# Attention products on pairs of 64x64 array tiles, and a triangle inversion by columns with unit steps on VectorE

## Chip, cores, metric

The kernel runs on one core of one Trainium2 chip. The metric is device time in microseconds, lower is better: 2314.84 us is the median of three runs of the kernel before (2313.5 to 2316.09). The words TensorE, VectorE, ScalarE, GpSimd and SyncE stand for the rows PE, DVE, ACT, POOL and SP of the profile; PEld is TensorE's weight load.

## What is computed

A layer in three parts; the first is a recurrence over 768 steps for 32 independent heads (4 batches of 8) of width 48.

```python
k_n = k / (np.linalg.norm(k, axis=-1, keepdims=True) + 1e-06)
for t in range(S):                      # S = 768
    y[:, :, t] = q_t @ state            # state: 48 x 48 for each of 32 heads
    v_old = state' k_t
    state = state + beta_t * outer(k_t, v_t - v_old)
x = y as (3072, 384)
P = exp(x @ w_gate), scaled 8 times over rows and columns; out = sum_e P[:, e] * (relu(x @ w1[e]) @ w2[e])
result = ((out @ a) * (out @ b) @ w3) @ w_out      # float64 weights
```

## The kernel before, in words

**Attention.** The 768 steps are cut into 12 chunks of 64. Two batches lie on the two halves of the 128 partitions (64 steps each), and the other 16 heads (`NG`) lie along the free axis, in two halves `hf` of 8. In a chunk the recurrence is a triangular system: `T' = (I + diag(beta) L)^-1 diag(beta)` is made from the products of keys, then `u = T'(v - K S)` and `S += K^T u`. Every value is kept as two fp16 parts, so each product is three matmuls (high x high, high x low, low x high). Because the two batches of a partition pair are independent, the stationary operand of such a product has to be block diagonal, 128 x 128 with two blocks of 64: the tiles `ktexp` (keys transposed), `ttexp` (T'), `kexp` (keys) and `bx` (u and state) hold zeros beside the blocks. They are filled in three ways: `ktexp` by copies on VectorE or ScalarE (`prep_k`, line 338 or 336), `ttexp`, `kexp` and `bx` by DMAs on SyncE's queue (line 363) from the compact tiles `tt16`, `k16`, `u16` and `s16`; the first chunk's `ttexp` and `bx` by copies.

**Order in a pair of chunks.** `prep_k` normalises the keys, splits them, transposes them on TensorE (`i,k` in the rows), and multiplies them with themselves (`gram`, rows `ktc,ktexp`). `invert(j)` inverts the 32 x 32 diagonal triangles of two chunks at once: 128 partitions, 32 triangles each after a 32 x 32 stream transpose (lines 620, 672, 674). It solves blocks of 8 by seven substitution steps (a product and a sum, lines 343 and 630), then joins blocks of 8 to 16 and of 16 to 32 by products with broadcast operands of 512 or 1024 elements followed by a sum (lines 343 and 643). The second operand of a product is read with a step of a whole row of 32. Four of the ten joins of a pair take their product on GpSimd. `tt_make` joins the two 32-halves of each 64-triangle with 32 x 32 TensorE tiles (rows `asys,g` and `stg,g`, `tile_position`) and makes `tt16`. `prep_q` makes the queries and `P^T` (rows `q,ktexp`). `seq(c)` is the recurrence: `ks` (rows `s,ktexp`), `um` (`r,ttexp`), `um2` (`u,kexp`) and `ym` (`q,bx` and `pt,bx`), with ScalarE and VectorE splitting what comes out of PSUM. The chunk's rows of x go to DRAM and back as `xr`.

**Filler and the rest.** `e0(c)` multiplies a finished chunk with the first expert's blocks (rows `xr,wA` and `hA,wA`, 256 columns): 144 matmuls a chunk for ten chunks. It has the lowest priority, so TensorE takes it where the attention waits. Then come the scaling of the gate (`sinkhorn`, lines 1048 to 1070), the other experts and the last layers, all matmuls of 256 to 512 columns.

**What sets the order.** A planner (`Plan.order`) lists all operations engine by engine from their data dependences, priorities, estimated costs and rings of buffers; each engine then runs its list in order. The single ring for `g12` makes a pair's `gram` wait for the `tt_make` of the pair before it, and the ring of two for x makes `e0(c)` finish before chunk c + 2 gets its x.

Of the kernel before, what the change touches and what calls it, by code (L numbers as in the profile page):

```python
# [17 lines left out]
NCH = 12  # L18
# [10 lines left out]
NKX = 1  # L29
NA0 = 2  # L30
NKC = 2
NBX = 2
# [3 lines left out]
NTC = 1  # L36
# [4 lines left out]
TSL = 1  # L41
ULAT = 1.0
# [5 lines left out]
DIRECT = 1  # L48
UDIRECT = 1
KX3 = 1  # L50
NG12 = 1
ZDVE = (("k16", 0), ("ktexp", 0))
ZPOOL = (("k16", 1), ("ktexp", 1))
# [3 lines left out]
class Ring:  # L57
    """Interchangeable buffers, each taken by one value at a time, with a cap per class of value."""
# [24 lines left out]
class Plan:  # L83
    """Operations with their data dependences; `order` lists them engine by engine with estimated costs."""
# [49 lines left out]
    def wait_for(self, o, e, pool, now, room):  # L134
        """Whether a more urgent operation will want the engine in a moment."""
        for x in pool:
            if x is o:
                return False
            if x.prio[0] < self.URGENT and e in x.rdy and len(x.engs) == 1 and now < x.rdy[e] <= now + self.AHEAD and x.engs[e] <= 2 * o.engs[e]:
                t = room(x)  # L140
                if t is not None and t <= now + self.AHEAD:
                    return True
        return False

    def order(self):
# [14 lines left out]
        def cost_of(o, e):  # L160
            """The tensor engine runs at half rate after a window of little work, until one of much work."""
# [148 lines left out]
class Kernel:  # L310
# [19 lines left out]
    # -- small helpers -------------------------------------------------  # L330
# [35 lines left out]
    # -- setup ---------------------------------------------------------  # L366
    def setup(self):
# [12 lines left out]
                  k16=((128, K16, 2, 2, 8, 64), F16), kexp=((128, NKX * 3584 + 16), F16), ktexp=((128, KSL, 2, 2, 8, 128), F16),  # L380
                  q16=((128, NQ, 2, 8, 64), F16), pt=((128, NPT, 2, 8, 64), F16),
                  ttexp=((128, TSL, 2, 2, 8, 128), F16), vs=((128, NV, NG, D), F32),
                  s16=((128, 2, 2, 8, D), F16), r16=((128, 2, 2, 8, D), F16), u16=((128, 2, 2, 8, D), F16),
                  bx=((128, NBX * 3584 + 16), F16))
        self.open("xst", "left", xst=((128, NY, 2, 512), F32))
        self.open("prep", "right",
                  kraw=((128, NG, D), F32), qraw=((128, NG, 64), F32), ktc=((128, NKC, 2, 8, 64), F16), tt16=((128, NTC, 2, 2, 8, 64), F16),
# [24 lines left out]
        def zero(name, i, key, n, prio):  # L412
            dst = lambda: self.wide(name)[:, i] if name in ("kexp", "bx") else T[name][:, i]
            if (name, i) in ZDVE:
                g.op({"DVE": n / 1900 + .07}, lambda e: nc.vector.memset(dst(), 0.0), w=[(key, i)], prio=prio)
            elif (name, i) in ZPOOL:
                g.op({"POOL": n / 1200 + .07}, lambda e: nc.gpsimd.memset(dst(), 0.0), w=[(key, i)], prio=prio)
            else:
                self.dma(lambda: dst().rearrange(FLAT), lambda: a["zeros"][:, 0:n], 256 * n, [], [(key, i)], prio)
        for i in range(K16):  # L420
            zero("k16", i, "kz", 2048, (-9, -8, 8, 8)[i])
        for i in range(KSL):
            zero("ktexp", i, "ktz", 4096, (-8.5, -7.5, 8, 9, 9)[i])
        for nm, n, key in (("kexp", NKX, "xz"), ("bx", NBX, "bz")):
            g.op({"POOL": .1}, lambda e, nm=nm, n=n: nc.gpsimd.memset(T[nm][:, 3584 * n:], 0.0), w=[(key, "z")], prio=1.3)
        for i in range(NKX):
            zero("kexp", i, "xz", 3584, 1.5)
        for i in range(TSL):
            zero("ttexp", i, "ttz", 4096, 1.4)
        for i in range(NBX):  # L430
            zero("bx", i, "bz", 3584, 1.6 + .1 * i)
# [7 lines left out]
        self.kxring = Ring(range(NKX), fifo=True)  # L439
        self.ktcring = Ring(range(NKC), fifo=True)  # L440
        self.bxring = Ring(range(NBX), fifo=True)
        self.stg = Ring(range(NST))
        self.kraw = Ring([0], fifo=True)
# [5 lines left out]
        self.ttring = Ring(range(TSL), fifo=True)  # L449
# [10 lines left out]
    # columns of `sml`  # L460
# [3 lines left out]
    def scale_chain(self, src, dst, inv, bits, prio, key):  # L464
        """From a column of row sums of squares: the power of two 2**bits over the root of their sum, and its inverse."""
# [22 lines left out]
    def vscan(self):  # L488
        """sv: power of two that bounds the scaled values and the state."""
# [12 lines left out]
    # -- attention, what does not depend on the state -------------------  # L502
    def prep_k(self, c):
# [3 lines left out]
        raw = ["asys"] if c == 1 else [("s16", hf, i) for hf in range(2) for i in range(2)] if c == 3 and KX3 else [self.kraw.new()]  # L507
        kraw = lambda: (T["asys"][:, 0:768] if c == 1 else T["s16"].rearrange("p h i y d -> p (h i y d)").bitcast(F32)).rearrange(
            "p (g d) -> p g d", d=D) if c == 1 or c == 3 and KX3 else T["kraw"]
# [33 lines left out]
        ktz = [("ktz", i) for i in range(KSL) if i == c or c >= KSL]  # L543
# [3 lines left out]
        for hf in range(2):  # L547
            gs = slice(8 * hf, 8 * hf + 8)
            kt = self.ktcring.new()
            for i in range(2):  # L550
                s = self.psum.new("attn")

                def tr(e, i=i, hf=hf, s=s):
                    o = self.ps(s, 4, 128)
                    for x in range(4):
                        self.mm(o[:, x], T["k16"][:, kc.at, hf, i, 2 * x:2 * x + 2].rearrange("p y d -> p (y d)"), T["i128"],
                                start=True, stop=True)
                g.op({"PE": 4 * .056}, tr, r=[(kc, "hl"[i], hf), "i128"], w=[s, (kt, i)], prio=pr)
                g.op({"ACT": act(512, True), "DVE": dve(512)},
                     lambda e, i=i, kt=kt, s=s: self.copy(e, T["ktc"][:, kt.at, i], self.ps(s, 8, 64)),  # L560
                     r=[s], w=[(kt, i)], prio=pr)
                for b in range(2):
                    r = slice(64 * b, 64 * b + 64)
                    g.op({"DVE": dve(512, 4), "ACT": act(512)},
                         lambda e, i=i, hf=hf, b=b, r=r, kt=kt: self.copy(
                             e, T["ktexp"][r, k.at, hf, i, :, 64 * b:64 * b + 64], T["ktc"][r, kt.at, i]),
                         r=[(kt, i)] + ktz, w=[(k, "t", hf, i, b)], prio=pr)
            s = self.psum.new("attn")

            def gram(e, hf=hf, s=s, kt=kt):  # L570
                o = self.ps(s, 8, 64)
                for x in range(8):
                    th, tl = T["ktexp"][:, k.at, hf, 0, x], T["ktexp"][:, k.at, hf, 1, x]
                    ch, cl = T["ktc"][:, kt.at, 0, x], T["ktc"][:, kt.at, 1, x]
                    self.mm(o[:, x], th, ch, start=True, stop=False)
                    self.mm(o[:, x], th, cl, start=False, stop=False)
                    self.mm(o[:, x], tl, ch, start=False, stop=True)
            g.op({"PE": 24 * .029}, gram, r=[(kt, 0), (kt, 1)] + [(k, "t", hf, i, b) for i in range(2) for b in range(2)],
# [932 lines left out]
```

## Time and profile before

| | |
|---|---|
| median of three runs | 2314.84 us (2313.5 to 2316.09) |
| span of the profiled execution | 2309.9 us |
| what lies around the span, taken from the median | 4.9 us |
| TensorE, VectorE, ScalarE, GpSimd busy | 2157.7, 1356.5, 711.7, 422.3 us |
| SyncE's queue (q1) | 292992 packets, 150.88 MB |

The page gives the span of one execution; its time from outside is not given apart, so the 4.9 us between span and median are used for it. Busy times are shares of the whole span, and the span has two very different stages: attention with filler up to about 500 us, then matmuls alone. A stage is therefore read from the windows, not from the page's totals. In the timeline a group of matmuls ends with the end of its last one, which is modelled; the time that a group takes from TensorE is from its start to the start of the next group.

### The profile page before, as it was taken

What the parts mean: (1) busy time and instruction counts of PE and PEld (TensorE: products, weight loads), DVE (VectorE), ACT (ScalarE), POOL (GpSimd) and SP (SyncE); (2) the same over time, 40 slices, a digit from 0 to 9 for tenths busy, and PEclk for the clock granted to TensorE, in tenths of its full rate; (3) what the DMA queues carried; (4) which work ended last, traced back from release to release, by engine and by line L of the source; (5) the groups of instructions that cost most, each with busy time, mean ns of one, the idle gap of its engine ahead of it and who ended that gap; (6) DMA issues with size and microseconds to landing.
All of it is one profiled execution on the core that took longest, in us unless ns stands there. A gap on an engine that the chain in (4) does not pass through costs nothing.

```text
span 2309.9 us, 38847 instructions
## 1 busy us (share of the span) xinstructions
PE 2157.7 (93%) x16055; PEld 1894.3 (82%) x16055; DVE 1356.5 (59%) x2350; ACT 711.7 (31%) x1415; POOL 422.3 (18%) x351
## 2 busy tenths in 40 slices
PE   2488888899999999999999999999999999999999
PEld 1477877789788888888888888888888888999999
DVE  8989888865877777777544444444444444222332
ACT  4645665554223222223121211212111111223332
POOL 5554456343211101111000000000000001300000
PEclk7579998999999999999999999999999999999999
DMA  6446545544523323233110101101010033500000
GB/s 218 123 90 108 107 94 115 87 97 151 172 87 119 107 79 108 93 113 112 53 42 19 42 27 33 46 14 46 14 46 28 18 127 101 110 18 18 15 15 21
DMA packets 312048, 175.10 MB, mean 76 GB/s; under 512 B 187072, under 2 KB 281600, under 8 KB 310848
## 3 DMA queue, kind: packets, MB, share of 16 engines
q1 hardware_dynamic: 292992, 150.88, 24.1%
q0 software_dynamic: 18880, 21.76, 3.7%
q8 instruction: 125, 2.05, 0.4%
q14 instruction: 51, 0.42, 0.1%
HBM read 123.09 MB, written 31.29 MB: 67 GB/s over the span
## 4 chain that ended last, share of the span: by engine, by line
PE 79%; DVE 14%; DMA 3%; issue 2%; ACT 1%; SPq 1%; POOL 0%; DVEq 0%; ACTq 0%; POOLq 0%
PE b L332 79%; DVE prod L343 3%; DMA ttexp<-tt 2%; DVE t L643 1%; DVE ktexp L338 1%; DVE xs L643 1%; DVE hA L346 1%; SPq L363 1%; DVE r L343 1%; DMA kexp<-k 0%; DVE xr L343 0%; DVE asys L672 0%; DMA pb<-p_d 0%; DVE stg L343 0%; DVE tt L343 0%
## 5 line engine op out<-in xcount | busy, mean ns | idle before, releaser
L332 PE MATMUL b<-xT,wA 128*128 128x512 f32 x2520 | 584.7, 389 | 0.0
L332 PEld LDWEIGHTS b<-xT,wA 128*128 128x128 f32 x2520 | 473.0, 188 | 98.2
L332 PE MATMUL b<-hA,wA 128*128 128x512 f32 (+1 forms) x2286 | 507.4, 361 | 16.1 <-DVE hA L346 15.9
L332 PEld LDWEIGHTS b<-hA,wA 128*128 128x128 f32 x2286 | 391.8, 194 | 78.8 <-DVE hA L346 18.4
L332 PE MATMUL b<-hB,wA 128*128 128x512 f32 (+1 forms) x1602 | 412.2, 384 | 1.0 <-DVE hB L346 1.0
L332 PEld LDWEIGHTS b<-hB,wA 128*128 128x128 f32 x1602 | 296.2, 189 | 60.8 <-DVE hB L346 1.8
L343 DVE TENSOR_TENSOR tmp<-b,pb 128x512 f32<-128x512 f32 x252 | 173.9, 690 | 243.4 <-PE b L332 242.7
L1179 ACT ACTIVATE hA<-b 128x512 fp32r<-128x512 f32 (+1 forms) x174 | 102.7, 590 | 635.3 <-PE b L332 627.8
L346 DVE SCALAR_TENSOR_TENSOR hA<-b,hA 128x512 fp32r<-128x512 f32 (+1 forms) x214 | 145.4, 680 | 179.2 <-ACT hA L1179 156.4
L332 PE MATMUL b<-xr,wA 128*128 128x256 f32 (+1 forms) x1368 | 248.3, 334 | 1.0 <-DVE ktc L338 1.0
L332 PEld LDWEIGHTS b<-xr,wA 128*128 128x128 f32 x1368 | 211.9, 199 | 21.1 <-DVE ktc L338 1.2
L332 PE MATMUL b<-xr,xT 128*128 128x256 f32 x1728 | 209.9, 283 | 0.0
L332 PEld LDWEIGHTS b<-xr,xT 128*128 128x128 f32 x1728 | 209.3, 192 | 0.0
L346 DVE SCALAR_TENSOR_TENSOR hB<-b,hB 128x512 fp32r<-128x512 f32 (+1 forms) x178 | 119.7, 674 | 150.9 <-ACT hB L1179 150.9
L343 DVE TENSOR_TENSOR acc<-acc,tmp 128x512 f32<-128x512 f32 x249 | 181.4, 728 | 6.6
L1179 ACT ACTIVATE hB<-b 128x512 fp32r<-128x512 f32 (+1 forms) x178 | 103.7, 583 | 194.4 <-PE b L332 193.4
L343 POOL TENSOR_TENSOR wA<-rawB,wA 128x768 fp32r<-128x768 f32 x13 | 26.8, 2064 | 659.4 <-ACT wA L336 659.4
L343 DVE TENSOR_TENSOR cv<-b,cv 128x256 f32<-128x256 f32 x96 | 40.7, 423 | 162.2 <-PE b L332 161.7
L343 POOL TENSOR_TENSOR cv<-cv 128x256 f32<-128x256 f32 (+1 forms) x68 | 53.2, 783 | 301.0 <-DVE cv L1276 179.6
L336 ACT ACTIVATE cvs<-cv 128x256 fp32r<-128x256 f32 x72 | 29.0, 402 | 168.4 <-DVE cv L346 168.4
L332 PEld LDWEIGHTS <-ktexp 128*128 128x128 f16 (+1 forms) x1680 | 58.3, 103 | 15.3 <-issue 8.2
L336 ACT ACTIVATE wA<-rawB 128x768 fp32r<-128x768 f32 x56 | 45.9, 841 | 78.6 <-DMA rawB<-in_moe_w 39.6
(191 smaller groups left out, 2247.2 us busy)
## 6 DMA issues: line engine op xcount, KB each, us to landing
pb<-p_d SPq DMA_DIRECT2D x90, 256.0 KB, 3.2
rawB<-in_moe_w SPq DMA_DIRECT2D x112, 192.0 KB, 3.1
w_d<-cvs SPq DMA_DIRECT2D x112, 128.0 KB, 2.5
cvr<-in_w3T SPq DMA_DIRECT2D x32, 256.0 KB, 3.3
xT<-w_d POOLq DMA_DIRECT2D x32, 256.0 KB, 3.5
vs<-in_v SPq DMA_DIRECT2D x18, 384.0 KB, 4.2
qraw<-in_qT SPq DMA_DIRECT2D x12, 512.0 KB, 3.9
cvr<-in_moe_w SPq DMA_DIRECT2D x24, 256.0 KB, 3.3
```

What stands on the lines that cost most here:

```text
L332: self.nc.tensor.matmul(*args, skip_group_check=True, **kw)
L336: self.nc.scalar.activation(out=out, in_=in_, func=AF.Copy, **({} if scale is None else {"scale": scale}))
L338: self.E[eng].tensor_copy(out, in_)
L343: self.E[eng].tensor_tensor(out=out, in0=in0, in1=in1, op=op)
L346: self.nc.vector.scalar_tensor_tensor(out=out, in0=in0, scalar=scalar, in1=in1, op0=op0, op1=op1)
L363: return self.g.op({eng: cost}, lambda _: e.dma_start(out=out(), in_=in_()), r=r, w=w, prio=prio, nbytes=nbytes, lat=lat)
L643: g.op({"DVE": dve(m)}, lambda e: nc.vector.tensor_reduce(out=out(), in_=pv(), axis=AX.X, op=ALU.add), r=[pb], w=wk, prio=pr)
L1179: g.op({"ACT": act(N, True)}, lambda e, s=s, h=h, hx=hx, N=N: nc.scalar.activation(out=self.hv(h, hx, N)[:, 0], in_=self.ps(s, N), func=AF ...
```

## The change

The stationary operands are not spread any more. A product is issued as two 64 x 64 tiles, one for each half of the partitions, on the array's tiles (0, 0) and (64, 64); both halves write the same PSUM bank, partitions 0 to 63 and 64 to 127. `ktexp`, `ttexp`, `kexp`, `bx` and `ktc`, their zeroing, copies and DMAs go; `kt` and `tt16` are read directly, `u16` and `s16` get two buffers each and 16 spare columns (what those give is not used). The inversion keeps the triangle `t` by columns (`p c i`) and the system by rows (`p i q`), so that both operands of a product are read with unit steps; all its products are on VectorE; three copies on ScalarE (`by_rows`) turn parts of `t`. `kraw` gets three buffers. The planner counts a pair of tiles as 0.036 us.

```diff
+    def three(self, o, lh, ll, rh, rl, first=True, last=True):
+        for l, r, st, sp in ((lh, rh, first, False), (lh, rl, False, False), (ll, rh, False, last)):
+            for p in range(2):
+                rows = slice(64 * p, 64 * p + 64)
+                self.mm(o(rows), l(rows), r(rows), start=st, stop=sp, tile_position=(64 * p, 64 * p))
...
                 def tr(e, i=i, hf=hf, s=s):
-                    o = self.ps(s, 4, 128)
-                    for x in range(4):
-                        self.mm(o[:, x], T["k16"][:, kc.at, hf, i, 2 * x:2 * x + 2].rearrange("p y d -> p (y d)"), T["i128"],
-                                start=True, stop=True)
+                    o = self.ps(s, 8, 64)
+                    for y in range(8):
+                        for p in range(2):
+                            r = slice(64 * p, 64 * p + 64)
+                            self.mm(o[r, y], T["k16"][r, kc.at, hf, i, y], T["i128"][r, r], start=True, stop=True, tile_position=(64 * p, 64 * p))
...
-                for b in range(2):
-                    r = slice(64 * b, 64 * b + 64)
-                    g.op({"DVE": dve(512, 4), "ACT": act(512)},
-                         lambda e, i=i, hf=hf, b=b, r=r, kt=kt: self.copy(
-                             e, T["ktexp"][r, k.at, hf, i, :, 64 * b:64 * b + 64], T["ktc"][r, kt.at, i]),
...
             g.op({"DVE": dve(4 * i * i)}, lambda e, pv=pv, i=i: nc.vector.tensor_reduce(
-                out=blk("t")[:, :, i, 0:i], in_=pv(), axis=AX.X, op=ALU.add), r=[pb], w=["t"], prio=pr)
+                out=blk("t")[:, :, 0:i, i], in_=pv(), axis=AX.X, op=ALU.add), r=[pb], w=["t"], prio=pr)
...
-            g.op({eng: dve(m) if eng == "DVE" else 2.72 * m / 1000 + .06}, lambda e: self.tt(
-                e, pv(), left().rearrange("p i (u q) -> p i u q", u=1).to_broadcast([128, ni, nc_, nq]),
-                right().rearrange("p q (c u) -> p u c q", u=1).to_broadcast([128, ni, nc_, nq]), ALU.mult),
+            g.op({"DVE": dve(m) + .08}, lambda e: self.tt(
+                "DVE", pv(), left().rearrange("p i (u q) -> p i u q", u=1).to_broadcast([128, ni, nc_, nq]),
+                right().rearrange("p (u c) q -> p u c q", u=1).to_broadcast([128, ni, nc_, nq]), ALU.mult),
...
+        def by_rows(p, n, o, rk):
+            g.op({"ACT": act(n * n) + .1}, lambda e: self.copy("ACT", rows(p, n), tm()[:, o:o + n, o:o + n].rearrange("p q i -> p i q")),
+                 r=rk + ka, w=["tr", ("tr", p)], prio=pr)
...
-        for b in range(2 if c >= DIRECT else 0):
-            r = slice(64 * b, 64 * b + 64)
-            self.dma(lambda r=r, b=b: T["ttexp"][r, tt.at, :, :, :, 64 * b:64 * b + 64].rearrange("p h i y d -> p (h i y) d"),
...
-                    three(o[:, y], T["ttexp"][:, tt.at, hf, 0, y], T["ttexp"][:, tt.at, hf, 1, y],
-                          T["r16"][:, 0, hf, y], T["r16"][:, 1, hf, y])
-            g.op({"PE": 24 * .025}, um, r=[("r16", 0, hf), ("r16", 1, hf)] + [(tt, b, hf) for b in range(2)],
+                    self.three(lambda r: o[r, y], tv(0, y), tv(1, y), rv(0, y), rv(1, y))
+            g.op({"PE": 24 * PAIR}, um, r=[("r16", 0, hf), ("r16", 1, hf)] + [(tt, i, hf) for i in range(2)],
...
-            expand(ux, "u16", [("u16", i, hf) for i in range(2) for hf in range(2)], pr + .4, ULAT)
```

**SyncE's queue in the middle of the attention.** This queue carries the loads of keys, values and queries and, before, the transfers that spread. Before, from one load of keys to the next:

```order
L363 DMA kraw<-in_k 128x768
L363 DMA ttexp<-tt_111 64x32x64 x2
L363 DMA bx<-u_99 64x32x48 x2
L363 DMA kexp<-k_90 64x16x48 x4
L363 DMA ttexp<-tt_111 64x32x64 x2
L363 DMA vs<-in_v 128x768
L363 DMA bx<-s_97 64x32x48
L363 DMA bx<-s_97 48x32x48
L363 DMA xs_d<-xst 48x8x128 x2
L363 DMA kraw<-in_k 128x768
```

Now:

```order
L358 DMA y_d<-yr 128x256 x6
L358 DMA xs_d<-xst 48x8x128 x2
L358 DMA kraw<-in_k 128x768
L358 DMA xst<-xs_d 128x6x128
L358 DMA vs<-in_v 128x768
L358 DMA qraw<-in_qT 128x1024
L358 DMA kraw<-in_k 128x768
```

Every transfer into `ttexp`, `bx` and `kexp` is gone; the loads and the round trip of x stay.

**VectorE in the second half of an inversion.** The rows with `prod` are products, those with `xs` or `t` the sums that follow. Before (a sum that reads `a_113` follows a product on GpSimd):

```order
L343 TENSOR_TENSOR prod<-asys,t 128x1024
L338 COPY ktexp<-ktc 64x8x64
L343 TENSOR_TENSOR xr<-xst,xr 128x768
L643 TENSOR_REDUCE xs<-prod 128x8x8
L343 TENSOR_TENSOR prod<-asys,t 128x1024
L643 TENSOR_REDUCE xs<-a_113 128x16x8
L643 TENSOR_REDUCE xs<-prod 128x8x8
L343 TENSOR_TENSOR prod<-t,xs 128x1024
L473 TENSOR_SCALAR sml<-b_135 128x1
L643 TENSOR_REDUCE t<-prod 128x8x8
L346 SCALAR_TENSOR_TENSOR hA<-b_136,hA 128x512
L643 TENSOR_REDUCE t<-a_113 128x8x8
```

Now (the products that read `a_109` read what ScalarE's `by_rows` copies left there):

```order
L338 TENSOR_TENSOR prod<-asys,t 128x1024
L333 COPY yr<-b_129 128x256
L616 TENSOR_REDUCE xs<-prod 128x8x8
L338 TENSOR_TENSOR prod<-asys,t 128x1024
L341 SCALAR_TENSOR_TENSOR hA<-b_128,hA 128x512
L616 TENSOR_REDUCE xs<-prod 128x8x8
L338 TENSOR_TENSOR prod<-asys,t 128x1024
L341 SCALAR_TENSOR_TENSOR hA<-b_134,hA 128x512
L616 TENSOR_REDUCE xs<-prod 128x16x8
L338 TENSOR_TENSOR prod<-a_109,xs 128x1024
L616 TENSOR_REDUCE t<-prod 128x8x8
L341 SCALAR_TENSOR_TENSOR hA<-b_129,hA 128x512
```

Six products of 1024 elements stand on VectorE for every pair of chunks instead of four, and the copies into `ktexp` between them are gone.

## Rows read from the trace of the kernel before

**Rows 1.** The page, parts 1 and 4: busy time by engine; shares of the last chain.

```profile
PE 2157.7 (93%) x16055; PEld 1894.3 (82%) x16055; DVE 1356.5 (59%) x2350; ACT 711.7 (31%) x1415; POOL 422.3 (18%) x351
PE 79%; DVE 14%; DMA 3%; issue 2%; ACT 1%; SPq 1%; POOL 0%; DVEq 0%; ACTq 0%; POOLq 0%
```

**Rows 2.** Windows: stretch, length, busy per engine, granted clock, DMA share, GB/s.

```profile
0.00:100.00 100.00, 33.42 (x592) 29.19 (x592) 89.22 (x150) 55.86 (x116) 55.70 (x45) 0.63 0.53 173
100.00:500.00 400.00, 327.22 (x5970) 308.46 (x5967) 342.58 (x520) 224.33 (x455) 203.01 (x129) 0.89 0.51 101
500.00:650.00 150.00, 140.72 (x1207) 127.09 (x1204) 99.43 (x185) 55.72 (x106) 43.02 (x35) 0.98 0.53 148
650.00:2309.00 1659.00, 1656.31 (x8301) 1429.57 (x8299) 825.24 (x1498) 375.79 (x739) 120.60 (x142) 1.00 0.19 57
```

**Rows 3.** Waits of TensorE, 0 to 500 us: us in total, times, longest.

```profile
PE b L332 <- DVE hA L346: 13.2, 8, 4.1
PE b L332 <- DVE asys L672: 13.0, 5, 5.9
PE b L332 <- DMA ttexp<-tt: 12.5, 7, 6.9
PE b L332 <- DMA bx<-u: 2.1, 2, 1.3
```

**Rows 4.** Timeline of TensorE: start, length, line, operation, out<-in, shape, count.

```profile
430.03 1.38 PE L332 MATMUL b<-u,kexp 128*128 128x48 f16 x48
431.25 0.86 PE L332 MATMUL b<-ktc,ktexp 128*128 128x64 f16 x24
431.95 1.38 PE L332 MATMUL b<-s,ktexp 112*128 112x48 f16 x48
...
337.28 1.05 PE L332 MATMUL b<-i,k 128*128 128x128 f16 x16
338.14 0.60 PE L332 MATMUL b<-hA,wA 128*128 128x256 f32 x3
...
533.51 2.32 PE L332 MATMUL b<-xr,wA 128*128 128x256 f32 x18
535.67 2.32 PE L332 MATMUL b<-hA,wA 128*128 128x256 f32 x18
```

**Rows 5.** The same, 32 x 32 tiles: at half clock, then at full clock.

```profile
74.30 2.77 PE L332 MATMUL b<-asys,g 32*32 32x32 f32 x96 [5.88 <-DVE asys L672]
77.22 1.06 PE L332 MATMUL b<-stg,g 32*32 32x32 f32 x32
...
480.88 1.71 PE L332 MATMUL b<-asys,g 32*32 32x32 f32 x96 [1.16 <-DVE asys L672]
482.52 3.64 PE L332 MATMUL b<-hA,wA 128*128 128x256 f32 x18
```

**Rows 6.** Groups of VectorE and GpSimd, 0 to 620 us: busy, mean ns, idle before.

```profile
L338 DVE COPY ktexp<-ktc 64x512 f16<-64x512 f16 x64 | 35.9, 563 | 1.4 <-ACT ktc L336 0.4
L343 DVE TENSOR_TENSOR prod<-asys,t 128x1024 f32<-128x1024 f32 x12 | 31.5, 2627 | 0.1
L343 DVE TENSOR_TENSOR prod<-t,xs 128x1024 f32<-128x1024 f32 x12 | 28.2, 2346 | 0.1
L343 DVE TENSOR_TENSOR prod<-t,xs 128x512 f32<-128x512 f32 x6 | 8.2, 1374 | 0.1
L343 DVE TENSOR_TENSOR prod<-asys,t 128x512 f32<-128x512 f32 x6 | 7.4, 1232 | 0.1
L343 DVE TENSOR_TENSOR prod<-t,asys 128x196 f32<-128x196 f32 x6 | 3.6, 601 | 0.1
L343 POOL TENSOR_TENSOR a<-asys,t 128x1024 f32<-128x1024 f32 x6 | 19.8, 3304 | 2.3 <-DVE t L643 2.3
```

**Rows 7.** Timeline of VectorE in the first inversion.

```profile
28.26 1.23 DVE L343 TENSOR_TENSOR a<-a,bm 128x1024 f32<-128x1024 f32 x1
51.08 1.93 DVE L343 TENSOR_TENSOR prod<-asys,t 128x1024 f32<-128x1024 f32 x1
62.79 3.27 DVE L343 TENSOR_TENSOR prod<-t,xs 128x1024 f32<-128x1024 f32 x1
```

More of the change, by code (lines that the diff above doesn't have):

```diff
@@ L47 @@
 HA = 2
[L48 to L50 removed]
 NG12 = 1
[L52 to L53 removed]
+PAIR = .036
+ZDVE = (0,)
+ZPOOL = (1,)
 FLAT = "p a b c d -> p (a b c d)"
@@ L568, in prep_k, with gram @@
+                g.op({"PE": 8 * PAIR}, tr, r=[(kc, "hl"[i], hf), "i128"], w=[s, (k, i, hf, "z")], prio=pr)
+                g.op({"ACT": act(512, True), "DVE": dve(512)},
+                     lambda e, i=i, hf=hf, s=s: self.copy(e, T["kt"][:, k.at, hf, i], self.ps(s, 8, 64)),
+                     r=[s], w=[(k, i, hf)], prio=pr)
             s = self.psum.new("attn")
-            def gram(e, hf=hf, s=s, kt=kt):
+            def gram(e, hf=hf, s=s):
                 o = self.ps(s, 8, 64)
[L572 to L577, printed above, removed]
@@ new lines, in invert @@
+        xt = lambda p, n: T["xs"][:, p * n * n:(p + 1) * n * n].rearrange("p (c q) -> p c q", c=n)
+        rows = lambda p, n: flat()[:, p * n * n:(p + 1) * n * n].rearrange("p (i q) -> p i q", i=n)
+        def by_rows(p, n, o, rk):
+            g.op({"ACT": act(n * n) + .1}, lambda e: self.copy("ACT", rows(p, n), tm()[:, o:o + n, o:o + n].rearrange("p q i -> p i q")),
+                 r=rk + ka, w=["tr", ("tr", p)], prio=pr)
+        for p in range(2):
+            by_rows(p, 8, 16 * p + 8, ["t"])
@@ new lines, in invert @@
+        for p in range(2):
+            o = 16 * p
+            prod(lambda p=p: xt(p, 8).rearrange("p c q -> p q c"), lambda o=o: am()[:, o + 8:o + 16, o:o + 8],
+                 lambda o=o: tm()[:, o:o + 8, o:o + 8], 8, 8, 8, ["asys", "t"], [("x8", p)])
+        for p in (1, 0):
+            o = 16 * p
+            prod(lambda o=o: tm()[:, o:o + 8, o + 8:o + 16].rearrange("p c i -> p i c"), lambda p=p: rows(p, 8),
+                 lambda p=p: xt(p, 8), 8, 8, 8, [("tr", p), ("x8", p)], [("t8", p)])
@@ new lines, in invert @@
+        out = lambda: tm()[:, 0:16, 16:32].rearrange("p c i -> p i c")
+        for c0 in (0, 8):
+            prod(lambda c0=c0: out()[:, 8:16, c0:c0 + 8], lambda: rows(0, 16)[:, 8:16, :], lambda c0=c0: xt(0, 16)[:, c0:c0 + 8, :],
+                 8, 8, 16, [("tr", 0), ("x16", 0, c0), ("x16", 8, c0)], [("t16", 1, c0)])
+        prod(lambda: out()[:, 0:8, :], lambda: rows(0, 16)[:, 0:8, 0:8], lambda: xt(0, 16)[:, :, 0:8],
+             8, 16, 8, [("tr", 0), ("x16", 0, 0), ("x16", 0, 8)], [("t16", 0)])
@@ L930, in seq @@
                 e, T["xst"][:, xb.at, hf], self.ps(s, 512), self.sc(28 + c)), r=[sy, ("sml", 28 + c)], w=[(xb, hf)], prio=pr + .5)
-        if c < NCH - 1:
-            self.SX = self.bxring.new()
-            expand(self.SX, "s16", [("s16", hf, i) for i in range(2) for hf in range(2)], pr + .4, 0.0)
         for b in range(2):
```

260 lines of the change are left out of this document (91 added, 169 removed).

## Prediction

> **What bounds the kernel now.** I read the page first, then the windows, TensorE's waits, its timeline, and VectorE's groups. The page shows TensorE busy 2157.7 of 2309.9 us and on 79% of the last chain [rows 1]. That is a sum over unlike stages, so the windows come next [rows 2]. From 650 us on TensorE is busy 1656.3 of 1659 us at a clock of 1.00: nothing of the change lies there, and that stage can only start earlier or later. All of TensorE's idle time is ahead of it: 66.6 us in the first 100, 72.8 us from 100 to 500, 9.3 us from 500 to 650. In the first stretch VectorE is busy 89 of 100 us and TensorE waits for the first inversion; from 100 to 500 VectorE is busy 342.6 of 400 us and TensorE 327.2. So the attention runs with two nearly full engines that take turns in waiting for each other. TensorE's waits name VectorE most often (13.2 us for `hA`, 13.0 us for the inverse), and 14.6 us the DMAs that spread `ttexp` and `bx` [rows 3].
>
> The end is therefore TensorE's work plus TensorE's idle time, and I make the sum that way: what the change adds to the work, what it takes from the idle time, what the clock does.
>
> **1. TensorE's work (adds).** Times are from the start of a group to the start of the next [rows 4], at full clock. A full-array product with 48 columns takes 25.4 ns (430.03 to 431.25, 48 of them), one with 64 columns 29.2 ns (431.25 to 431.95, 24), a transposing one with 128 columns 53.8 ns (337.28 to 338.14, 16). By the order there are 1632, 2256 and 192 of these: 41.5 + 65.9 + 10.3 = 118 us. The change issues 8544 tile matmuls, 4272 pairs, of 48 (1632 pairs) or 64 columns (2640 pairs). What a pair costs no row shows. The nearest rows are the 32 x 32 tiles, which also alternate between the two halves of the partitions and write one bank: 96 of them take 1.64 us at full clock, 17.1 ns each, 34.2 ns for two [rows 5]. That is the low end: 4272 x 34.2 = 146 us, +28. The high end is no overlap of the two tiles, each at the price of a full-array product: 1632 x 50.8 + 2640 x 58.4 = 237 us, +119. I take 36 ns, close to the tile rows since they are the same kind of instruction, with a little for the longer stream: 154 us, **+36**.
>
> A rule speaks against this. The 32 x 32 rows show two row groups writing one bank at 17.1 ns an instruction, less than any full-array product above [rows 5]. The Trainium skill (TensorEngine Tiling (Array Packing), Restrictions and Gotchas) says that different row tiles cannot access the same PSUM bank at the same time, and both tiles of a pair here write one bank. By that rule the pairs would cost the high end; where the rows can be compared, they do not bear it out.
>
> **2. TensorE's idle time (takes).** VectorE loses the copies into `ktexp`, 35.9 us [rows 6]. In the inversions 24 products of 1024 took 31.5 + 28.2 = 59.7 us and 12 of 512 took 15.6 us [rows 6]. With unit steps I price them by the only product of that size with a contiguous operand, 1.23 us for 1024 [rows 7], and 0.65 us for half as much: 29.5 + 7.8, a gain of 38 us. The 12 products of 1024 and 12 of 512 that leave GpSimd come back on VectorE: +22.6 us. The small substitution products (0.60 us at 196 elements) I take at 1 us less per inversion, 6 us. Together VectorE does 36 + 38 - 23 + 6 = 57 us less. GpSimd loses 19.8 us of 1024-products alone [rows 6], and with them some of the times when a VectorE instruction is stretched: a product of 1024 took 1.93 us at one place and 3.27 us at another [rows 7].
>
> Of that, 100 to 500 us gets about five sixths, 48 us: VectorE's load falls from 342.6 to about 295, below TensorE's. The DMA waits (14.6 us) vanish with the DMAs. I take the idle time there from 72.8 to 30 us, **-43**: 14.6 from the DMAs, the rest from the waits for VectorE and GpSimd [rows 3]. Ends: 14.6 alone, or 60. In the first 100 us the first `um` waits for keys, one inversion and the copies into `ktexp` and `ttexp`; with about 2.5 us less in four large products, 3 us of copies ahead of it and as much behind, and shorter stretched steps I take **-12** (5 to 25).
>
> Against this stand new waits. VectorE's products with `by_rows` operands wait for three ScalarE copies a pair, queued in order behind evacuations of filler; ScalarE is busy only 224 of 400 us [rows 2], and three waits of a microsecond in six inversions would be 18 us of VectorE, not of TensorE. At the end, cover is lost: 504 filler matmuls stood behind the last `um`, now 288 do. At 120 ns each (533.51 to 535.67, 18 of them) [rows 4] that is 26 us less to hide the gate's scaling, which runs on VectorE between small matmuls. The next expert's blocks can fill most of it; I take **+5** (0 to 20). The zeroing, 110 spreading DMAs and their place in SyncE's queue I cost at nothing beyond the waits named; loads of keys, values and queries behind them can only start earlier.
>
> **3. The clock (takes).** A granted clock of 0.89 over 400 us is 88 us at the lower level, 1.2 GHz; at 82% busy and half speed that loses some 36 us [rows 2]. In the first stretch (0.63) filler starts only when the first chunk is done, so an earlier start also ends that cold stretch earlier. Fewer waits should give about half of this back: **-20** (from -30 to +30, since tile products may do the opposite, see the second rival).
>
> **Sum.** 2309.9 + 36 - 43 - 12 + 5 - 20 = 2276 us of span. The 4.9 us around the span, which link it to the median of 2314.84, give 2281 us; I say **2280 us**, 1.5% faster. A measurement of this kernel can tell 0.2%, some 4.6 us, from no change.
>
> **Rivals.**
> - *The tiles do not overlap.* Each pair costs two products: +119 instead of +36, and with TensorE then fuller the idle time falls no further: about 2280 + 83 - 8 = 2355 us, slower. It decides in the attention products; the gains of 70 us are used up at a pair price of (118 + 70) / 4272 = 44 ns. For it: at half clock the 32 x 32 tiles take at most 28.9 ns each (96 in 2.77 us) [rows 5], and 32 columns alone are 26.7 ns at 1.2 GHz, so those rows fit one tile after the other too, if an fp32 instruction passes 32 columns once. Against: 17.1 ns is well under the 25.4 ns of a product with 48 columns, and the fp32 product appears as two instructions, which fits two slower passes running side by side as well. The skill's rule above would give this time. Chance 0.18.
> - *The clock falls.* The stretch at full clock with 32 x 32 tiles at 480.88 follows a wait, and such products fill little of the array [rows 5]. If pairs of 64 x 64 tiles leave the grant as low as 0.80 from 100 to 500 us, half-speed time grows from 88 to 160 us, and 72 x 0.82 x 0.5 = 30 us are lost instead of 20 gained: 2330 us. For it: the grant is low in the stretch in which products are small. Against: that stretch also has all the waits. Chance 0.08.
> - *Unit steps gain nothing.* If a product's price is its broadcast operand and not the step, the 36 products of 1024 stay at some 2.4 us and those of 512 at 1.3 us; VectorE then does 36 + 6 us less but 36 x 1.2 = 43 us more for what came from GpSimd and the rest, so nothing is gained there, and only the DMA waits, the startup and the clock's smaller half remain: 2314.8 + 36 - 14.6 - 12 + 5 - 10 = 2319 us, no change or barely slower. Against: 1.23 us was measured with a broadcast operand too (`bm`) [rows 7]. Chance 0.08.
> - *Better than forecast.* Pairs at 34 ns and the idle time at 20 us: 2280 - 8 - 10 - 12 = 2250 us. Chance 0.12.
>
> **How the numbers follow.** The forecast, with its bounds on idle time and clock, has 0.48, the better case 0.12, and a weaker form of the forecast (new waits, 2290 to 2319 us) 0.06. The three rivals have 0.18, 0.08 and 0.08. Faster by over 0.2%: 0.48 + 0.12 + 0.05 = 0.65. Within 0.2%: 0.09, from the weaker form and the third rival. Slower: 0.26, the first two and the rest. The range takes the better case and its bounds below, and the second and third rival above, and most but not all of the first: 2240 to 2345 us. The likeliest case alone spans 2255 to 2305 us.
>
> **What would show it.** In the profile after: in TensorE's timeline 24 pairs in 0.86 us at full clock (36 ns each); 24 pairs in 1.2 us or more is the first rival. Products of 1024 near 1.23 us on VectorE; 2.3 us is the third. From 100 to 500 us TensorE busier than VectorE, a grant of 0.92 or more (0.80 is the second), no wait for a DMA. The stage at full load should start some 35 us earlier than now and last as long. The forecast is wrong if the attention's end moves little although VectorE's load falls: then the planner's order or a new wait sets the pace.

## Result, and the profile after

The change makes the kernel **slower by 0.64%**: 2327.41 us (median of four runs, 2326.55 to 2332.47) against 2314.17 us for the kernel before, ratio 1.0064 with a 95% interval of 1.0051 to 1.0077. The forecast was 2280 us and faster. The profiled execution has a span of 2324.9 us, 15 us more than before [rows 1].

The page after, part 1, and two queues of part 3:

```profile
PE 2191.2 (94%) x20519; PEld 1926.3 (83%) x20519; DVE 1325.7 (57%) x2312; ACT 696.5 (30%) x1398; POOL 335.2 (14%) x324
...
q1 hardware_dynamic: 115920, 127.82, 17.8%
...
q8 instruction: 160, 2.62, 0.5%
```

VectorE has 31 us less to do, GpSimd 87 us less, SyncE's queue 23 MB less. TensorE is busy 33.5 us longer. The windows after, columns as in [rows 2]:

```profile
0.00:100.00 100.00, 36.46 (x1245) 33.91 (x1246) 81.80 (x136) 54.95 (x117) 46.26 (x44) 0.62 0.43 137
100.00:500.00 400.00, 359.64 (x9238) 340.50 (x9235) 307.89 (x487) 207.11 (x430) 127.89 (x103) 0.91 0.20 59
500.00:650.00 150.00, 123.98 (x1680) 109.94 (x1679) 99.01 (x171) 54.72 (x106) 37.39 (x31) 0.86 0.43 125
650.00:2324.00 1674.00, 1671.13 (x8367) 1441.92 (x8365) 837.03 (x1521) 379.77 (x746) 123.64 (x146) 1.00 0.19 58
```

TensorE's idle time is now 63.5, 40.4, 26.0 and 2.9 us, before 66.6, 72.8, 9.3 and 2.7: 18.6 us less in all. So 33.5 us more busy time less 18.6 us of idle time make the 15 us. The idle time has new owners. TensorE's waits, 0 to 650 us (us in total, times, longest):

```profile
PE b L327 <- DVE asys L650: 28.0, 2, 26.5
PE b L327 <- issue: 25.5, 28, 1.5
PE b L327 <- ACT q L721: 13.4, 2, 8.6
PE b L327 <- DVE cs L995: 10.8, 5, 4.0
```

The DMA waits of [rows 3] are gone. In their place stand 25.5 us "<- issue", 28 gaps of at most 1.5 us in which TensorE waits for nothing that the profile shows. Where they lie is plain from TensorE's timeline:

```profile
261.59 0.31 PE L327 MATMUL b<-stg,g 32*32 32x32 f32 x6
262.33 0.60 PE L327 MATMUL b<-stg,g 32*32 32x32 f32 x26 [0.43 <-issue]
262.85 1.70 PE L327 MATMUL b<-u,k 64*64 64x48 f16 x96
264.39 0.26 PE L327 MATMUL b<-q,s 64*64 64x64 f16 x6
266.06 0.28 PE L327 MATMUL b<-pt,u 64*64 64x64 f16 x6 [1.40 <-issue]
...
268.05 0.22 PE L327 MATMUL b<-q,s 64*64 64x64 f16 x2
269.51 0.25 PE L327 MATMUL b<-q,s 64*64 64x64 f16 x4 [1.24 <-issue]
...
270.43 1.29 PE L327 MATMUL b<-s,kt 64*64 64x48 f16 x70
273.24 0.77 PE L327 MATMUL b<-s,kt 64*64 64x48 f16 x26 [1.52 <-issue]
```

From gap to gap there are 128 matmuls: 26 + 96 + 6 from 262.33, and as many from 266.06 and from 269.51 (the rows left out are groups of six). The gaps cut groups in two (6 and 26, 2 and 4, 70 and 26), so no operand is being waited for. The page's q8 row fits: 2.62 MB in 160 packets are 16 KB each, and 20519 / 160 = 128 matmuls a packet. Before, 16055 matmuls came in 125 packets, again 128 each:

```profile
q8 instruction: 125, 2.05, 0.4%
```

TensorE runs dry of **instructions**. While they are there, a pair costs what was hoped: 96 tiles in 262.85 to 264.39, 32 ns a pair.

What stands in line behind the gaps shows in VectorE's timeline of the same place:

```profile
265.48 0.55 DVE L341 SCALAR_TENSOR_TENSOR s<-b,s 128x384 f16<-128x384 f32 x1
271.40 0.56 DVE L341 SCALAR_TENSOR_TENSOR vs<-b,vs 128x384 f32<-128x384 f32 x1 [5.37 <-PE b L327]
274.05 0.56 DVE L341 SCALAR_TENSOR_TENSOR vs<-b,vs 128x384 f32<-128x384 f32 x1 [2.08 <-PE b L327]
```

VectorE waits 7.5 us for two groups of `ks`; this line alone waits 22.5 us between 100 and 500 us. The products of the inversion did become cheap, as VectorE's groups from 0 to 620 us show against [rows 6]:

```profile
L338 DVE TENSOR_TENSOR prod<-asys,t 128x1024 f32<-128x1024 f32 x18 | 27.0, 1502 | 0.5
L338 DVE TENSOR_TENSOR prod<-a,xs 128x1024 f32<-128x1024 f32 x18 | 22.9, 1270 | 0.5
```

**The stretch that pays.** The attention alternates between an inversion and the stretch from its end (the transpose at line 650, before 672) to the start of the next (590, before 620), in which the recurrence and the next keys run. The windows of these stretches, before (the second, third and fifth of five):

```profile
162.00:190.00 28.00, 26.51 (x638) 25.33 (x635) 21.28 (x46) 18.41 (x43) 7.22 (x6) 0.87 0.39 71
241.00:268.00 27.00, 26.01 (x611) 24.21 (x612) 21.55 (x44) 20.43 (x48) 12.61 (x10) 1.00 0.32 65
...
410.00:436.00 26.00, 23.62 (x594) 22.46 (x595) 19.19 (x37) 16.40 (x37) 3.65 (x5) 0.93 0.31 47
```

And after (all but the first):

```profile
169.00:210.00 41.00, 35.97 (x1329) 33.52 (x1325) 22.78 (x47) 24.99 (x55) 8.99 (x9) 0.67 0.21 59
250.00:289.00 39.00, 33.74 (x1290) 31.95 (x1290) 25.03 (x56) 23.93 (x53) 11.51 (x11) 0.82 0.24 68
340.00:378.00 38.00, 33.39 (x1335) 30.86 (x1336) 20.75 (x43) 25.53 (x58) 6.27 (x7) 0.82 0.18 54
418.00:462.00 44.00, 40.13 (x1466) 37.69 (x1461) 23.55 (x46) 27.02 (x58) 11.02 (x11) 0.81 0.16 43
```

The five stretches add up to 203 us, before 157. The inversions got shorter (by the starts and ends of those lines 274 us for six, before 293), but the stretch with twice the matmuls got longer by more. About 1330 matmuls are 10 packets; ten packets in 39 us are 3.9 us each. Before, 600 matmuls made five packets in 27 us, and nothing ran dry.

The gaps are one part of this growth and not all of it. Of the 46 us, TensorE's busy time makes 35 (173.4 us in the five stretches, before 138.7) and its idle time 11. Within the idle time, 21 us of gaps put down to issue stand where other waits stood before. The busy time goes with twice as many instructions and with a lower grant: 0.67 to 0.82 in all five, where before only the first (0.59) and the second (0.87) were under 0.9. How it divides between the two was not tested.

### The profile page after: what moved, and what is told of

The parts are those of the page before. It is cut to its first block, busy times and chain, and to the rows that moved or that the text cites. A ratio compares the mean times of both kernels' runs of the same rounds, so it can differ in the third digit from the quotient of the medians.

```text
span 2324.9 us, 47410 instructions
## 1 busy us (share of the span) xinstructions
PE 2191.2 (94%) x20519; PEld 1926.3 (83%) x20519; DVE 1325.7 (57%) x2312; ACT 696.5 (30%) x1398; POOL 335.2 (14%) x324
## 3 DMA queue, kind: packets, MB, share of 16 engines
q8 instruction: 160, 2.62, 0.5%
## 4 chain that ended last, share of the span: by engine, by line
PE 74%; DVE 2%; issue 1%; DMA 0%; ACT 0%; POOL 0%; SPq 0%; DVEq 0%; ACTq 0%; POOLq 0%
PE b L327 74%; DVE acc L338 1%; DVE p L341 0%; DVE p L338 0%; DMA xst<-xs_d 0%; DMA rawB<-in_moe_w 0%; DMA xs_d<-xst 0%; DVE cs L995 0%; DVE xT L338 0%; DVE rs L991 0%; DVE tmp L338 0%; DVE rs L992 0%; DVE cv L1205 0%; DVE hA L341 0%; DVE cv L341 0%
## 5 line engine op out<-in xcount | busy, mean ns | idle before, releaser
L327 PE MATMUL b<-hA,wA 128*128 128x512 f32 (+1 forms) x2322 | 499.1, 356 | 3.9 <-DVE hA L341 3.1
L327 PE MATMUL b<-hB,wA 128*128 128x512 f32 (+1 forms) x1566 | 406.1, 387 | 0.0
L327 PE MATMUL b<-xr,wA 128*128 128x256 f32 (+1 forms) x1368 | 238.7, 327 | 2.6 <-ACT wA L331 2.2
L327 PEld LDWEIGHTS b<-xr,wA 128*128 128x128 f32 x1368 | 204.6, 193 | 24.1 <-ACT wA L331 2.6
L338 POOL TENSOR_TENSOR wA<-rawB,wA 128x768 fp32r<-128x768 f32 x17 | 33.0, 1939 | 674.7 <-ACT wA L331 674.7
L327 PEld LDWEIGHTS <-kt 64*64 64x64 f16 x3360 | 71.1, 123 | 21.3 <-issue 16.9
```

What stands on the lines that cost most here:

```text
L327: self.nc.tensor.matmul(*args, skip_group_check=True, **kw)
L338: self.E[eng].tensor_tensor(out=out, in0=in0, in1=in1, op=op)
```

## Experiments

Twelve kernels ran. Times are medians, with the ratio to the kernel before on the same chip.

**1. Each half of the change alone.** `e1_inverse_only` is the kernel before with the new `invert`; `e2_pairs_only` is the changed kernel with the old one.

> The kernel before with only the new inversion (by columns, unit steps, VectorE alone); the attention products stay on spread 128-row operands. Theory A, the tile pairs are the losing part (the instruction stream of the tiles runs TensorE dry, 25.5 us of idle time in 28 gaps of up to 1.5 us, and VectorE then waits 22.5 us for the state products): this kernel is faster than before, 2295 to 2310 us, and shows no gaps of that kind. Theory B, the inversion is the losing part (VectorE now carries the products that GpSimd carried): this kernel is at 2320 us or more.

> The changed kernel with the inversion of before put back (strided products, part of them on GpSimd); the tile pairs stay. Theory A: the loss stays, 2325 us or more, with some 25 us of gaps put down to issue. Theory B: the loss goes, 2300 to 2314 us.

Measured: e1 2308.97 us, ratio 0.9984 [0.9973, 0.9995]; e2 2345.93 us, ratio 1.0149 [1.0128, 1.0170]. Theory A holds: the pairs cost 1.5%, the new inversion takes back 0.85% beside them and is worth 0.16% alone. e1 has 1.1 us "<- issue", e2 30.0 us. That e1 gains so little of VectorE's 24 us was not followed up; its stretches between inversions shrank from 157 to 115 us, and the inversions, with more of the other work now inside them, grew from 293 to 332.

**2. The instruction stream by itself.** A kernel that only streams products of zeros (`tiles` goes round the diagonal of the array, tile by tile, `fill` issues full products of 512 columns):

```diff
+            fill(96)
+            tiles("pair", 1024, 64)
+            fill(96)
+            for i in range(1024):
+                y = i % 8
+                mm("full", b["full"][:, 48 * y:48 * y + 48], w["full"], x["full"][:, 48 * y:48 * y + 48])
+            fill(96)
+            for _ in range(32):
+                tiles("mixed", 32, 64)
+                fill(6)
+            fill(96)
+            tiles("quad", 1024, 32)
```

> Only streams of matrix products on zeros, with nothing to wait for; none of the reference is computed. 1024 tiles of 64x64 by 48 columns in pairs; 1024 full 128x128 by 48; 1024 tiles in groups of 32 with 6 fillers of 512 columns behind each; 1024 tiles of 32x32 by 48 in fours. Theory A (instructions come 128 matmuls at a time, one packet in 3.5 to 3.9 us at best): the pair stream takes 28 to 31 us, with a gap put down to issue behind every 128 matmuls; the stream of 32x32 tiles takes as long; the full one 26 to 29 us; the mixed one shows no gaps and prices a pair at about 33 ns. If the gaps of the changed kernel have another cause (a semaphore or a buffer that the profile doesn't name), the pair stream runs through in about 17 us (512 pairs of 32.5 ns) without a gap.

Its timeline on TensorE:

```profile
23.33 4.23 PE L32 MATMUL bpair<-xpair,wpair 64*64 64x48 f16 x255
28.24 2.21 PE L32 MATMUL bpair<-xpair,wpair 64*64 64x48 f16 x128 [0.68 <-issue]
31.70 2.21 PE L32 MATMUL bpair<-xpair,wpair 64*64 64x48 f16 x128 [1.25 <-issue]
35.42 2.21 PE L32 MATMUL bpair<-xpair,wpair 64*64 64x48 f16 x128 [1.52 <-issue]
...
89.12 3.39 PE L32 MATMUL bfull<-xfull,wfull 128*128 128x48 f16 x128 [0.61 <-issue]
...
120.11 0.69 PE L32 MATMUL bmixed<-xmixed,wmixed 64*64 64x48 f16 x32
120.73 1.47 PE L32 MATMUL bfill<-xfill,wfill 128*128 128x512 f16 x6
122.13 0.69 PE L32 MATMUL bmixed<-xmixed,wmixed 64*64 64x48 f16 x32
...
212.25 1.46 PE L32 MATMUL bquad<-xquad,wquad 32*32 32x48 f16 x128 [1.99 <-issue]
215.71 1.47 PE L32 MATMUL bquad<-xquad,wquad 32*32 32x48 f16 x128 [1.99 <-issue]
```

There is nothing to wait for, and still a gap stands behind every 128 matmuls once the first 255 are through. The period is mostly 3.46 or 3.72 us, now and then 4.00, whether the 128 matmuls fill 2.2 us of it or 1.5. From 28 to 50 us, six of these periods, the chip's DMA engines move nothing for this core but six packets:

```profile
q8 instruction: 6, 0.10, 1.9%
```

The pair stream takes 26.8 us (28 to 31 expected, 17 without a limit); the quads are no faster, 26.0 us. So a matmul costs at least 27 ns in a long run, a pair 54 ns, whatever the array could do. The full products, 25.4 ns apart before, are just at this limit: gaps of 0.61 us. With filler between them no gap is left. This is what the spread operand bought: one instruction for both halves.

**3. Instructions against array time.** Both kernels are the changed one with its plan and order; the third of the three products is left out, or moves one column.

```diff
 # e9_two_products
-        for l, r, st, sp in ((lh, rh, first, False), (lh, rl, False, False), (ll, rh, False, last)):
+        for l, r, st, sp in ((lh, rh, first, False), (lh, rl, False, last)):
 # e10_third_thin
-                self.mm(o(rows), l(rows), r(rows), start=st, ...)
+                n = 1 if l is ll else r(rows).shape[-1]
+                self.mm(o(rows)[:, 0:n], l(rows), r(rows)[:, 0:n], start=st, ...)
```

> The changed kernel with its plan and its order as they are, but the third product (low part of the weights by the high part of the moving operand) is left out of every attention group: 2848 of 8544 tile products fewer, 1424 pairs or 46 us of array time at 32.5 ns. Theory S (between two inversions TensorE's instructions come too slowly: 1300 to 1500 products in stretches of 37 to 45 us, ten packets of 128 at 3.5 to 3.9 us): the stretches shorten by the 3.5 packets that are missing, 10 us each or more, and the time falls to 2265 to 2290 us; gaps put down to issue under 10 us. Theory R (the recurrence is bound by its chain of operations on ScalarE and VectorE, and tiles lie beside it): the stretches shorten by 3 us or less, 2305 to 2320 us.

> As e9_two_products, but the third product stays as an instruction and moves 1 column instead of 48 or 64, so that nearly all of its array time is gone and all instructions are there (all but its first column of the third product is left out). Theory S: the instructions cost what they cost before, the stretches between inversions stay within 3 us of the changed kernel's (37 to 45 us), the gaps put down to issue grow to 25 us or more, 2318 to 2330 us. If it is the array's time that counts: the same as e9_two_products within 4 us.

Measured: e9 2287.35 us, ratio 0.9885 [0.9867, 0.9903]; e10 2348.33 us, ratio 1.0147 [1.0129, 1.0165]. The stretches of e9 (first and third):

```profile
76.00:113.00 37.00, 27.62 (x1002) 25.77 (x1002) 24.55 (x48) 25.05 (x56) 16.98 (x15) 0.60 0.25 68
...
236.00:268.00 32.00, 28.67 (x1017) 26.62 (x1016) 25.59 (x56) 24.69 (x56) 11.62 (x11) 0.84 0.28 82
```

The same stretches of e10:

```profile
74.00:117.00 43.00, 37.90 (x1300) 36.11 (x1302) 26.86 (x49) 25.53 (x55) 16.81 (x15) 0.50 0.21 59
...
257.00:296.00 39.00, 35.59 (x1272) 33.86 (x1272) 25.05 (x56) 23.99 (x53) 12.64 (x11) 0.70 0.23 68
```

With a third of the tile instructions gone, the five stretches add up to 169 us; with the instructions kept and only their columns gone, 212, against 203 in the changed kernel. Work on VectorE and ScalarE is about the same in all three, so theory R, the chain on those engines, is out; what counts is the number of instructions. e9's time and gaps (7.6 us) came as expected, its stretches shortened by 4 to 8 us each and not by 10.

The two kernels do not tell the supply of instructions from the array's time, though, because e10 took no time off the array. Of each six tiles in a row of its timeline, two move one column and four move 64:

```profile
271.50 0.26 PE L327 MATMUL b<-pt,u 64*64 64x64 f16 x6 [1.35 <-issue]
271.59 0.26 PE L327 MATMUL b<-q,s 64*64 64x64 f16 x6
```

From 271.50 to 272.73 there are 13 such rows, 0.095 us each; in the changed kernel 20 rows of six full tiles, from 266.06 to 267.95, also take 0.095 us each. A row takes no longer with 64 columns in all six tiles than with one column in two of them, 16 ns a tile. So e10 left TensorE as much to do as the changed kernel has, and e9 saved the array's time together with the instructions: its span is 42 us shorter, TensorE is busy 44 us less (2147.1 us against 2191.2), and its idle time hardly differs, although the gaps fell by 18 us. The limit of the supply itself is shown by the stream kernel and by the gaps at every 128th matmul.

e10 missed its numbers: gaps put down to issue are only 10.7 us, the time lies 21 us above the changed kernel's, and one stretch grew by 4 us instead of at most 3. The reason shows in its windows:

```profile
100.00:500.00 400.00, 378.57 (x9093) 361.11 (x9088) 287.26 (x470) 203.76 (x422) 127.84 (x103) 0.77 0.20 57
```

The granted clock fell to 0.77, from 0.91. At the lower level three pairs take 0.16 us (517.70 to 517.86 in the changed kernel's timeline), 53 ns a pair and 3.4 us a packet: about as long as a packet takes to come, so the gaps close without anything being gained. Of the 21 us, 9 lie in the stretches and 12 in the inversions (286 us for six instead of 274), in which the filler then runs at the lower clock too.

**4. The plan's price and its order.** The changed kernel with another price of a pair in the plan (`PAIR`), and with the pair groups marked `low=True`, so that filler is put between them.

> The changed kernel with the price of a pair in the plan raised from 0.036 to 0.054 us (128 matmuls in 3.5 us, the shortest spacing that the trace shows between two packets of TensorE's instructions); the same instructions, in another order. If the plan's wrong price is what makes VectorE stand in line behind late state products (22.5 us for the vs line between 100 and 500 us), that wait falls to under 12 us and the time to 2312 to 2322 us. If the gaps themselves are the cost, whatever the plan believes: 2323 to 2332 us, gaps still about 25 us.

> The changed kernel with the price of a pair in the plan at 0.033 us, what the trace measures at full clock, instead of 0.036: the same instructions in a slightly other order. It tells how far the time hangs on the plan's order alone. If the loss belongs to the instructions: 2318 to 2336 us. If the order that the plan happened to give is at fault: under 2312 us.

> As e11_price33 with 0.040 us in the plan. If the time follows the plan's price of a pair (0.054 gave 2370 us): 2332 to 2345 us; if orders only scatter: 2318 to 2336 us.

> The changed kernel with the groups of tile pairs marked as low, so that the plan lets them have TensorE for at most 1.2 of 3.4 us while there is other work for it: expert 0's filler goes between the groups. If the gaps put down to issue are paid because the tiles stand close together (25.5 us in 0 to 650), they fall under 12 us. If filler between the tiles is as good as free, the time falls to 2305 to 2320 us; if the filler is then missed behind the inversions and the recurrence becomes longer by the filler in it, the time stays at 2322 to 2340 us although the gaps are gone.

| | time, us | ratio | "<- issue", us |
|---|---|---|---|
| 0.033 | 2325.05 | 1.0047 [1.0032, 1.0063] | 28.5 |
| 0.036, the change | 2327.41 | 1.0064 [1.0051, 1.0077] | 25.5 |
| 0.040 | 2342.14 | 1.0119 [1.0103, 1.0136] | 30.2 |
| 0.054 | 2370.05 | 1.0236 [1.0217, 1.0256] | 33.0 |
| 0.036, low | 2412.55 | 1.0424 [1.0404, 1.0444] | 12.5 |

None of these orders comes near the kernel before, so nothing speaks for the order that 0.036 happened to give being at fault. The time follows the plan's price upwards; with the price of a pair in a dense run (0.054) it is far above both of e3's ranges. VectorE's wait at the `vs` line fell to 8.7 us there, as the first of them wanted, and the time rose all the same: the five stretches between inversions now add up to 254 us. Why the plan makes them so long was not followed further. e5 halves the gaps (12.5 us, where under 12 was expected) and loses 85 us: its waits tell where.

```profile
PE b L327 <- DVE asys L650: 91.9, 6, 29.9
...
PE b L327 <- issue: 12.5, 14, 2.4
```

The filler that hides the gaps is the filler that stood behind the inversions, and in the recurrence it is no free guest: the stretches between inversions grow to 64 to 70 us. The direction of the second branch held, its size (2322 to 2340 us) was far too small. Spreading the tiles out halves the gaps and costs more than it gains; of the changed kernel's variants only the one with fewer instructions (e9) is clearly faster.

**5. Added instructions, a failed pair.** On e1's kernel, one tiny product of zeros behind each attention product, or one of 112 columns behind every six:

```diff
 # e6_tiny
+        self.mm(o[0:32, 0:1], self.T["i128"][0:32, 32:64], self.T["i128"][0:32, 32:33], start=False, stop=True, tile_position=(0, 0))
 # e8_wide
+        if self.npad % 6 == 0:
+            self.mm(self.now[:, 0:112], self.T["i128"][0:64], self.T["i128"][0:64, 64:65].to_broadcast([64, 112]), start=False, stop=True)
```

> The spread products with the new inversion (as in e1_inverse_only), and behind each of the 4272 attention products one more product of a 32x32 block of zeros with one column, which adds nothing to the result: TensorE then has as many instructions as the changed kernel. If the supply of instructions costs the time, gaps put down to issue appear (15 us or more in 0 to 650) and the time is at least 8 us above that of e8_wide. If only the array's time counts, it equals e8_wide within 4 us and shows no gaps.

> As e6_tiny, with the same orders on all engines, but the additional array time lies in 712 products of 112 columns of zeros (one behind every six, some 47 ns each by the 53.8 ns of a product of 128 columns, 33 us in all) instead of 4272 tiny ones (some 8 ns each in the stream of 32x32 tiles, 35 us). No gaps put down to issue above 2 us; 2315 to 2335 us by the 33 us of array time, of which what falls behind inversions is free.

Measured: 3231.61 us, ratio 1.3957 [1.3937, 1.3977], and 2457.13 us, ratio 1.0621 [1.0604, 1.0638]. Both expectations were missed, and neither kernel tests the supply: the zeros used part of the array and the products all of it, and every change between the two costs time of its own. Against e1 that is 923 us for 4272 added products and 148 us for 712, some 0.2 us for each in both. (e8's products also change the values that the layer gives.) The timeline of e6, in which the clock is at its lower level:

```profile
300.11 0.24 PE L332 MATMUL b<-q,ktexp 128*128 128x64 f16 x1
300.27 0.18 PE L332 MATMUL b<-i 32*32 32x1 f16 x1
300.38 0.24 PE L332 MATMUL b<-q,ktexp 128*128 128x64 f16 x1
```

0.27 us for what should be two short instructions. In the stream kernel at full clock 32 tiles and 6 fillers take 2.02 us (120.11 to 122.13); the tiles alone are 0.51 (128 in about 2.03), six fillers 1.30 (96 in 20.73 us, 50.18 to 70.91), so two changes cost 0.21 us, 0.1 us each.

**6. Fewer pairs where they pay most.** e1's kernel with tile pairs only in `um`, which removes the DMAs into `ttexp`, 576 of the 4272 products:

```diff
-                    three(o[:, y], T["ttexp"][:, tt.at, hf, 0, y], T["ttexp"][:, tt.at, hf, 1, y],
-                          T["r16"][:, 0, hf, y], T["r16"][:, 1, hf, y])
+                    for i, x, st, sp in ((0, 0, True, False), (0, 1, False, False), (1, 0, False, True)):
+                        for p in range(2):
+                            r = slice(64 * p, 64 * p + 64)
+                            self.mm(o[r, y], T["tt16"][r, tt.at, hf, i, y], T["r16"][r, x, hf, y],
+                                    start=st, stop=sp, tile_position=(64 * p, 64 * p))
```

> The kernel before with the new inversion, and only the product of T' with the right side on tile pairs (576 of 4272 products), which takes away the 22 copies that spread T' by DMA and the waits for them (12.2 us in e1_inverse_only). If these waits lie on the recurrence and 576 tile pairs are too few to run the instruction stream dry, the time is 2295 to 2306 us. If the waits only move to the next late operand, 2306 to 2312 us.

Measured: 2300.73 us, ratio 0.9945 [0.9928, 0.9962], the fastest full version, 13.9 us under the kernel before in the same job. Its window in the middle of the attention:

```profile
100.00:500.00 400.00, 350.42 (x6541) 331.12 (x6537) 336.41 (x565) 218.15 (x461) 141.76 (x108) 0.91 0.41 86
```

6541 matmuls from 100 to 500 us instead of 9238, and 2.5 us "<- issue" up to 650 us. With 576 pairs among spread products the gaps stay at 2.5 us, with all 4272 they come to 25.5. How much of the gain over e1 (ratios 0.9945 and 0.9984) is the waits for `ttexp` was not separated.

## Why the prediction was wrong

**TensorE's work, +36: the size held, the price in a long run did not.** TensorE is busy 33.5 us more, where this term and the clock's together gave 16. Of the 33.5, 4272 pairs at 32 ns make 137 us against 118, +19 (the dearest group of the stretch shown above, 96 tiles from 256.88 to 258.69, comes to 38 ns a pair); 110 changes between tiles and full products ahead of 650 us (before 56), at 0.1 us, make about +5; the rest goes with the lower clock. This split is an estimate. The first rival, tiles that do not overlap, is out: 32 ns a pair in one bank, where no overlap was to cost 50.8 ns or more.

The Trainium skill (TensorEngine Tiling (Array Packing), Restrictions and Gotchas) says that different row tiles cannot access the same PSUM bank at the same time. The trace does not bear that out in this form: the two tiles write different partitions of one bank, at 32 ns a pair.

The rival's threshold was the right one to watch all the same. It said that the gains are used up at 44 ns a pair; in a long run a pair costs 54, for a reason that none of my cases held.

**The failed step** is in part 1: "What a pair costs no row shows", and then "I take 36 ns". I bounded the pair by the array and stayed close to the low end, which came from [rows 5], runs of 96 tiles, less than one packet. The number of instructions, 20519 instead of 16055, stood in no term. The runs show in its place a supply of one packet of 128 matmuls in 3.46 us or more, 54 ns a pair, and 25.5 us in which TensorE waits for it. What sets the pace of the packets was not tested. The forecast was 34 us less of span, the measurement 15 us more; the gaps are 25.5 of these 49 us. They are also more than the 15 us: without them, and if nothing else took their place, the change would be some 10 us faster than the kernel before, which is an estimate that no run shows. The other half of the 49 us is 17.5 us of busy time, where the clock's term failed (below), and 6 us of other waits. The sign that the prediction named for this came true: the attention's end did not come earlier although VectorE's load fell, and a new wait is there.

The page before could have warned: 125 packets for 16055 matmuls, 128 each. No full-array product there is cheaper than 25.4 ns [rows 4], and 128 of those are 3.25 us, close under the packet's 3.46; but that pace itself stood in no row.

**Idle time, -43 from 100 to 500 us: it came to -32.** The DMA waits went, as said, and VectorE's load fell from 342.6 to 307.9 us instead of 295. The new gaps of 25.5 us are most of the difference over all stretches (forecast -43 - 12 + 5 = -50, measured -18.6). What the sum could not see is that the same stream lengthens the stretch between inversions, in which VectorE then waits.

**The first 100 us, -12: it came to -3.** The first inversion ended at 76 us, no earlier than before: it started 4 us earlier and took 6 us longer (51 us against 45), which stays unexplained; TensorE waits 26.5 us in one piece for its `asys`.

**The tail, +5: it came to +17.** The attention ends 13 us later (last gate product at 555 instead of 542 us), and the scaling of the gate takes 39 us, before 33. The lost cover was named. In it a few VectorE steps that mostly take 0.36 us stretched to 2.7 us:

```profile
566.85 2.70 DVE L341 SCALAR_TENSOR_TENSOR p<-p,cs 128x192 f32<-128x192 f32 x1
...
572.17 0.36 DVE L341 SCALAR_TENSOR_TENSOR p<-p,cs 128x192 f32<-128x192 f32 x1
```

GpSimd ran subtractions for `xT` and issued DMAs at that time; that these are the cause was only argued.

**The clock, -20: nothing came.** 0.91 instead of 0.89 from 100 to 500 us, but 0.86 instead of 0.98 behind. So the clock shortened TensorE's work nowhere by as much as it lengthened it behind 500 us. The second rival (0.80) did not happen in the changed kernel, but in e10 it did: the same instructions with a third of the tiles cut to one column, and the grant is 0.77. What lowered the grant behind 500 us was not tested.

**The third rival** (unit steps gain nothing) is out, as far as the products go: products of 1024 fell from 2.35 and 2.63 us to 1.27 and 1.50, and beside the pairs the new inversion takes 0.85% off (e2 against the change).

## What to carry to other kernels

Count TensorE's instructions, not only its columns. Divide the matmuls of the stretch that sets the pace by 128: if the packets times 3.5 us come near its length, splitting a product into smaller tiles can make it slower even where the array does each tile for half the price. Zeros in a block-diagonal operand can then be cheaper than a second instruction, as here, and tiles paid where they removed a wait (e7), a few at a time.

## What the runs showed of the hardware that was not expected

- TensorE gets its instructions in packets of 16 KB, 128 matmuls with their weight loads. In a dense run one came every 3.46 to 4.00 us, 27 to 31 ns a matmul, and the wait for it is called "issue" in the profile (e4: 9.3 us in 1024 pair tiles, 14.7 us in 1024 of 32 x 32).
- A change between tiles and full products costs TensorE about 0.1 us at full clock (e4).
- A 64 x 64 tile takes 16 ns at full clock and 27 ns at the lower one (six in 0.095 and in 0.16 us). Cutting two of each six to one column, as e10 does, changed neither.
- The grant stayed at 1.00 in the pair stream, busy 17.5 of 26.8 us, and fell to 0.56 over the stream of 32 x 32 tiles, busy 11.3 of 26.0 us.
- In the profiled execution of e11 the grant was 1.00 in the first 100 us (0.62 in the changed kernel's), and its time hardly differs, 2325.05 us: that stretch is set by the first inversion and not by TensorE.
